# Transposing q on VectorE instead of TensorE in a pooled-attention and mixture-of-experts kernel

## The chip, the cores and the metric

The kernel runs on one core of a Trainium2 chip. The core has four compute engines: TensorE (PE in the profile, with its weight loads as PEld), VectorE (DVE), ScalarE (ACT) and GpSimd (POOL). A fifth one, SyncE (SP), issues nearly all transfers between the main memory and the on-chip memory (SBUF); 16 DMA engines carry them out. Matmul results go to eight banks of PSUM, 2 KB per partition each.

The metric is the time of one execution on the device in microseconds (us). Runs of this kernel before the change took 172.65, 172.67 and 173.02 us.

## What is computed

Batch 8, 8 heads, 576 tokens, 64 values a head. Attention with pooled keys and values feeds a layer of four attention experts, of which each token uses two. Shortened:

```python
# attention: 576 queries against 72 pooled keys
k_p = k.reshape(B, H, 72, 8, 64).mean(axis=3)
v_p = v.reshape(B, H, 72, 8, 64).mean(axis=3)
attn = softmax(q @ k_p.T / 8)
x = heads_side_by_side(attn @ v_p)            # (8, 576, 512)
# experts: causal attention in each, two experts a token by the gate
logits = x @ w_gate                           # (8, 576, 4)
for e in range(4):
    q, k, v = x @ wq[e], x @ wk[e], x @ wv[e]
    ye = softmax(causal(q @ k.T / 8)) @ v @ wo[e]
    out += gate_weight[e] * ye                # 0 where e is not among the two
```

## The kernel before

Each batch's 576 tokens are split into 512 main tokens and a tail of 64; the tails of two batches are put together in one tile of 128 rows. Work is cut into small units, each a function, named `batch:unit`. A text of names (`ORDER`, line 21) is the order in which the units are emitted, and every engine runs its instructions in that order. A unit can yield: its first appearance in the text emits its matmuls, the next one what reads their result (an exponential, a copy), and a third one what follows. So the text fixes the order within every engine's queue and, by the order of allocation, who gets which buffer.

The units of one batch, in the order of the data:

- `lk`, `lq`, `lv` load k, q, v of the main tokens (lines 312 to 319), four tokens to a partition, all eight heads, 1 MB each; batch 0 loads in four pieces and batch 1 in two (`CUTS`, line 77). `lkt`, `lqt`, `lvt` load the tails (lines 321 to 337). q's tails of two batches go into one tile, `qtail`.
- `ks`, `vs` add pairs of tokens (`sums`, on GpSimd or VectorE), `kp` and `vp` finish the pooling with a constant matrix on TensorE (`pool_k`, `pool_v`). `kp` leaves pooled keys with the 64 values of two heads in the 128 partitions, 72 pooled tokens in the columns.
- `qc` casts q to bf16 (`cast_q`, line 354): GpSimd from batch 2 on, VectorE and ScalarE for batches 0 and 1.
- `q0` to `q3` (`q_t`, line 396), one for each pair of heads: four TensorE transposes of 128x128 into a PSUM tile of the pool `ps1`, then a VectorE copy to `qT`. Batches 6 and 7 (`COPY_IN_ORDER`) reorder tokens in that copy.
- `s0` to `s3` (`scores`, line 419), one for each pair of heads: two matmuls that contract 64 rows each, in the upper and the lower half of the array, into one two-bank tile of the pool `ps2`; then one ScalarE exponential of 72x1024 into `etA`.
- `a0` to `a3` (`av`): the exponentials times the pooled values, and the division on VectorE, into `x_tm`. `x0` to `x3` (`x_t`) transpose that on TensorE against `perm`, an identity with its columns reordered, since the tokens come four to a partition. Batches 6 and 7 let DMA transpose (`xd`).
- `p` and `v` project to the experts' queries, keys and values, `g1` to `g6` make the gate weights, `c..` are the experts' scores and exponentials, `o` their outputs, `t` transposes, `w`, `y`, `z` the output projection and the store.
- Odd batches have a part for the two tails (`part_t`, line 756): `qt` casts q's tails on GpSimd, `qx` transposes them on TensorE, `sx` makes 16 score matmuls of 64 rows and 64 columns into one `ps2` tile and one exponential, and then `ax`, `xx`, `pt`, `vx`, `hd`, `h0`, `h1`, `ox`, `tx`, `w4` follow like the main units.
- `W:l.` and `W:c.` load and cast the weights. `W:h0` to `W:h31` (`busy`, line 287) are 32 pairs of matmuls on zeros whose result nobody reads.

`ps1` has two buffers of one bank, `ps2` three of two banks; together they are all of PSUM. `ps2` serves the scores of both attentions, the products with the values and `v`; `ps1` serves everything else. A unit that takes a buffer waits until the last reader of its former content is done.

Of the kernel before, what the change touches and what calls it, by code (L numbers as in the profile page):

```python
# [8 lines left out]
FP32 = mybir.dt.float32  # L9
BF16 = mybir.dt.bfloat16  # L10
ADD = mybir.AluOpType.add
# [10 lines left out]
W:h21 W:h22 W:h7 0:lk3 W:h3 0:lq3 0:lkt 0:ks3 0:kt 0:qc3d 0:lk2 W:h18 0:lk0 W:h14 W:h16 0:lv1 W:h27  # L22
0:lvt 0:qc3a W:h28 0:lq0 W:h13 0:kp3 0:lq2 0:lk1 W:h30 0:q3 0:vs1 1:lq1 0:lq1 0:kp3 0:qc0a 1:lkt
0:ks2 W:h12 W:h25 0:vt 1:qc1a 0:qc0d 0:lv2 0:q3 0:s3 0:qc2a W:h4 0:s3 0:qc1a 0:vs2 0:ks0 0:kp2 W:h9
W:h1 0:kp2 0:ks1 1:qc1d 0:qc2d 0:kp0 0:lv3 W:h26 0:kp1 0:kp0 W:h19 0:lv0 W:h15 0:kp1 0:q0 0:vs0 W:h5
0:qc1d 0:q2 0:q0 1:lq0 W:h8 0:q2 1:kt 0:vs3 0:q1 1:q2 0:q1 0:s0 0:s1 0:s0 0:s2 1:lk1 0:vp 1:q2 0:s2
1:lk0 1:lvt 0:vp 1:ks1 0:lqt W:h23 1:lv1 1:q3 0:a0 1:lv0 0:a2 1:q3 W:lk 1:qc0d 1:ks0 1:lqt W:h6 0:s1
0:a1 1:vt W:lq 0:a2 0:a0 1:qc0a 0:a1 W:h29 1:q1 W:h11 W:h17 W:h2 1:q1 1:kp1 1:kp0 1:kp1 1:vs0 1:kp0
0:a3 1:q0 0:a3 1:s2 1:qt 1:s1 1:q0 W:lv 0:x0 1:s0 1:s2 0:x2 2:lq 1:s1 1:s3 2:qc 1:s0 0:x0 W:c1 0:x2
0:x1 W:h10 W:h0 1:vs1 W:h20 W:h24 1:s3 0:x3 0:x1 1:vp 0:x3 W:c3 0:p1 2:lkt 1:vp W:c2 0:p1 1:qx 1:qx  # L30
1:a1 1:a3 1:a0 W:c0 0:p3 1:a1 1:sx 1:a3 0:p3 W:cv 2:kt 0:p0 1:a0 2:lk 1:a2 0:p2 0:v2 1:a2 1:sx 0:v0
0:p0 1:x3 0:p2 0:c2 1:x1 0:v2 0:c2 0:c11 0:v0 1:x3 1:x2 0:c11 0:c2 0:c10 1:x1 2:lv 2:lvt 1:x2 0:g1
0:c00 0:g2 0:c11 2:q0 2:q0 1:x0 1:x0 1:ax 2:q1 2:q1 1:ax 1:p1 1:p2 0:c00 0:c01 2:ks 3:lk 0:g3 0:g4
1:v2 3:lkt 1:p1 2:q3 1:v2 2:vs 2:q3 1:p2 2:lqt 2:kp 0:c01 1:v0 3:lqt 1:xx 2:kp 0:g5 3:lq 2:vt 3:lvt
2:s1 0:c10 0:c10 1:xx 2:s1 1:v0 2:s0 2:q2 1:vx 2:q2 2:s0 2:s3 2:s3 0:g6 2:s2 2:s2 3:lv 2:vp 4:lq
0:c00 1:vx 1:g1 0:o1 1:g2 2:vp 1:p3 2:a1 1:g3 2:a2 0:o1 3:ks 3:qt 0:c01 2:a1 1:p3 1:pt 2:a2 4:lkt
2:a0 1:p0 3:kt 1:pt 2:a3 2:a0 2:a3 4:lk 4:lvt 3:qx 1:g4 1:hd 1:h0 3:qx 3:qc 1:p0 1:hd 3:kp 1:h0
1:c11 3:kp 1:c2 2:x2 2:x1 3:vs 2:x2 3:vt 4:lv 1:c11 2:x1 0:o0 1:c2 2:x0 0:o0 2:x3 1:c00 2:x0 3:sx
2:x3 1:c00 1:c10 3:q2 3:q3 3:sx 2:v2 4:qc 3:q2 3:q3 0:t1 5:lq 1:c10 1:g5 3:q1 0:t1 4:kt 3:q1 3:s3
2:v2 2:v0 0:t0 2:v0 3:s3 3:s1 3:s2 0:t0 3:q0 3:s1 1:h1 3:vp 3:q0 2:p1 3:s2 1:hd 4:lqt 3:vp 3:s0  # L40
7:lkt 1:c01 4:q2 2:g1 1:h1 2:g2 1:c00 2:p1 4:q2 3:s0 3:a1 5:lkt 2:p0 4:q1 1:c2 3:a1 4:ks 4:q1 3:a3
2:p0 3:ax 2:p3 1:c11 1:c01 2:p3 3:a3 4:q3 2:c01 4:vt 2:c00 5:lk 1:c01 2:c01 4:q3 4:q0 3:ax 2:p2 1:g6
3:a0 4:q0 3:a0 5:lqt 4:kp 2:p2 4:kp 3:a2 4:vs 2:c00 1:ox 5:qc 3:xx 1:c10 3:a2 3:xx 4:s1 4:s0 1:o0
3:x1 1:ox 3:x3 3:x1 4:s1 3:x3 W:lo 4:s3 4:s0 4:s3 3:x0 4:vp 3:x0 5:ks 3:pt 3:pt 4:s2 4:vp 5:kt 2:c11
4:s2 3:x2 2:c00 5:q2 2:g3 1:o0 3:x2 2:c11 1:o1 3:p3 4:a3 5:q2 5:q3 3:p3 3:hd 5:lv 5:lvt 1:o1 2:c2
# [24 lines left out]
5:y2 7:c10 5:y2 7:pt 5:y1 5:y2 7:c2 7:c01 7:pt 5:y0 7:o1 7:g5 5:w4 7:c01 5:y0 7:g6 7:h1 5:w3 7:o1  # L70
7:c00 6:y1 5:w3 6:y1 7:c00 7:o0 6:w0 7:h1 7:t1 7:h0 5:y0 7:o0 5:w3 7:t1 7:hd 6:w0 7:t0 6:y1 7:hd
# [12 lines left out]
COPY_IN_ORDER = (6, 7)  # L84


@with_exitstack
def kernel(
    ctx: ExitStack,
    tc: tile.TileContext,  # L90
    q: bass.AP,
    k: bass.AP,
    v: bass.AP,
    moe_w_gate: bass.AP,
    moe_wq: bass.AP,
    moe_wk: bass.AP,
    moe_wv: bass.AP,
# [6 lines left out]
    POOLW = 8  # L104
# [917 lines left out]
```

## Time and profile before

| | |
|---|---|
| median of three runs | 172.67 us (172.65 to 173.02) |
| span of the profiled execution, first to last instruction | 171.8 us |
| HBM read, written | 30.42 MB, 9.44 MB |
| transfers | 52712 packets, 21712 of them under 512 B |
| TensorE, VectorE, ScalarE, GpSimd busy | 160.6, 124.3, 125.1, 100.8 us |

A profile is taken from one execution, whose instructions span a little less than the time that is measured for the run. Rows of instructions start with their start and length in microseconds, then engine, line, operation, `output<-inputs`, shapes and `x` the number of instructions merged in the row; in brackets stands how long the engine had been idle before, and what ended that. All instructions carry the line of the helper that emits them, L134, so they are told apart by their tiles. Rows of groups give the busy time and the mean of one instruction in ns, then the idle time before them and who ended it.

TensorE's rows need care: matmuls are pipelined, and each is shown with its whole latency. A matmul of 128 columns is shown with 219 ns. What it costs in a stream is the time from its start to the start of the next.

### The profile page before, as it was taken

How to read it: one execution, taken by the hardware profiler on the slowest of the kernel's cores; microseconds unless marked ns; L12 is line 12 of the kernel's file. 1: busy time of each engine (PE TensorE's matmuls, PEld its weight loads, DVE VectorE, ACT ScalarE, POOL GpSimd, SP SyncE). 2: the span in 40 equal slices, each digit the busy share in tenths (PEclk: the TensorE clock that was granted, in tenths of full speed). 3: DMA queues.
4: the chain of work that ended last, by engine and by line, in shares of the span. 5: the costliest groups of instructions: out<-in, count | busy, mean ns of one | idle time of the engine just before them, and what ended most of it. 6: DMA issues, size and time to landing. Idle time of an engine off the chain costs nothing.

```text
span 171.8 us, 5246 instructions
## 1 busy us (share of the span) xinstructions
PE 160.6 (94%) x2064; PEld 101.7 (59%) x2090; DVE 124.3 (72%) x358; ACT 125.1 (73%) x176; POOL 100.8 (59%) x222
## 2 busy tenths in 40 slices
PE   7968999899999999999999999999999999999990
PEld 2424544465767756777677667765665767456550
DVE  6465695858588786888768887878688658657861
ACT  2004717878787978679989759985998797798841
POOL 8402643157999969999962996891234133668200
PEclk9999999999999999999999999999999999999999
DMA  4999999999999999999939967641348355576966
GB/s 140 262 342 335 306 301 257 332 335 329 216 321 347 332 332 301 295 287 334 302 82 341 360 216 201 230 126 61 67 122 275 65 125 156 210 216 132 333 253 208
DMA packets 52712, 42.03 MB, mean 245 GB/s; under 512 B 21712, under 2 KB 47824, under 8 KB 52688
## 3 DMA queue, kind: packets, MB, share of 16 engines
q1 hardware_dynamic: 52608, 41.57, 82.8%
q8 instruction: 16, 0.26, 0.7%
q10 hardware_dynamic: 80, 0.13, 0.4%
q14 instruction: 8, 0.07, 0.2%
HBM read 30.42 MB, written 9.44 MB: 232 GB/s over the span
## 4 chain that ended last, share of the span: by engine, by line
PE 75%; DVE 7%; ACT 6%; DMA 4%; SPq 3%; issue 2%; DVEq 0%; ACTq 0%
PE p_ps L134 14%; PE v_ps L134 8%; PE y_ps L134 7%; PE sB_ps L134 5%; PE oB_ps L134 5%; PE sA_ps L134 4%; PE qT_ps L134 4%; DMA qraw<-in_q_dram 4%; PE idle_ps L134 4%; PE oA_ps L134 4%; PE xT_ps L134 3%; SPq L134 3%; PE oBt_ps L134 3%; PE vp_ps L134 2%; PE pt_ps L134 2%
## 5 line engine op out<-in xcount | busy, mean ns | idle before, releaser
L134 ACT ACTIVATE etA<-sA_ps 72x1024 bf16<-72x1024 f32 x32 | 31.3, 1018 | 10.7 <-PE sA_ps L134 10.5
L134 PE MATMUL p_ps<-xT,wqk 128*128 128x512 bf16 x114 | 31.5, 379 | 1.5 <-ACT qk L134 0.6
L134 ACT ACTIVATE etB<-sB_ps 128x1024 bf16<-128x1024 f32 x32 | 32.2, 1025 | 0.2 <-PE sB_ps L134 0.2
L134 POOL TENSOR_SCALAR_AFFINE_SELECT etB<-etB 128x256 bf16<-128x256 bf16 x48 | 18.8, 410 | 12.2 <-ACT etB L134 11.8
L134 POOL TENSOR_TENSOR vsum<-vraw 128x512 bf16<-128x512 f32 (+2 forms) x18 | 18.3, 1041 | 9.9 <-DMA vraw<-in_v_dram 9.8
L134 ACT CAST qk<-p_ps 128x512 bf16<-128x512 f32 x32 | 18.5, 586 | 7.6 <-PE p_ps L134 6.8
L134 DVE TENSOR_TENSOR x_tm<-oA_ps,rzA 128x512 bf16<-128x512 f32 x32 | 22.1, 692 | 1.1
L134 PE MATMUL idle_ps<-idle 128*128 128x512 bf16 x61 | 18.2, 414 | 3.1 <-DVE kp L134 1.3
L134 PEld LDWEIGHTS <-wqk 128*128 128x128 bf16 x192 | 14.7, 98 | 10.4 <-issue 1.1
L134 DVE COPY qT<-qT_ps 128x512 bf16<-128x512 bf16 x32 | 15.4, 487 | 6.2 <-PE qT_ps L134 5.9
L134 POOL TENSOR_TENSOR ksum<-kraw 128x512 bf16<-128x512 f32 (+1 forms) x16 | 18.0, 1146 | 2.3 <-DMA kraw<-in_k_dram 2.3
L134 PE MATMUL y_ps<-wo_t,oT 128*128 128x512 bf16 x57 | 16.7, 379 | 0.2
L134 PE MATMUL v_ps<-wvg,xT 128*128 128x260 bf16 x128 | 16.8, 274 | 0.0
L134 ACT COPY ofin<-y_ps 128x512 f32<-128x512 f32 x20 | 11.6, 587 | 6.4 <-PE y_ps L134 1.7
L134 POOL CAST qbf<-qraw 128x2048 bf16<-128x2048 f32 x6 | 11.4, 1897 | 5.6 <-ACT etT L134 5.5
L134 PEld LDWEIGHTS <-xT 128*128 128x128 bf16 x128 | 11.9, 97 | 3.1 <-issue 0.4
L134 PEld LDWEIGHTS <-etA 72*128 72x128 bf16 x256 | 11.0, 97 | 4.3 <-DVE x_tm L134 0.4
L134 PE MATMUL sB_ps<-qk 64*128 64x512 bf16 (+3 forms) x128 | 13.2, 299 | 0.0
L134 PEld LDWEIGHTS <-etB 128*128 128x128 bf16 x256 | 11.3, 97 | 2.5 <-POOL etB L134 0.6
L134 DVE COPY xT<-xT_ps 128x512 bf16<-128x512 bf16 x24 | 9.7, 420 | 4.1 <-PE xT_ps L134 3.8
L134 PE MATMUL oB_ps<-vaug,etB 128*128 128x65 bf16 x256 | 12.4, 193 | 0.1
L134 PE MATMUL qT_ps<-ident,qbf 128*128 128x128 bf16 x128 | 12.2, 219 | 0.3
(125 smaller groups left out, 329.8 us busy)
## 6 DMA issues: line engine op xcount, KB each, us to landing
out_dram<-ofin SPq DMA_DIRECT2D x28, 256.0 KB, 2.7
qraw<-in_q_dram SPq DMA_DIRECT2D x6, 1024.0 KB, 9.9
kraw<-in_k_dram SPq DMA_DIRECT2D x6, 1024.0 KB, 9.8
vraw<-in_v_dram SPq DMA_DIRECT2D x6, 1024.0 KB, 8.2
kraw<-in_k_dram SPq DMA_DIRECT2D x4, 256.0 KB, 4.9
qraw<-in_q_dram SPq DMA_DIRECT2D x4, 256.0 KB, 5.4
ktail<-in_k_dram SPq DMA_DIRECT2D x8, 128.0 KB, 7.1
vraw<-in_v_dram SPq DMA_DIRECT2D x4, 256.0 KB, 6.2
```

The costliest lines, as they stand in the source:

```text
L134: return tc.keep_in_program_order(fn(*args, **kwargs))
```

## The change

- q is loaded with 18 consecutive tokens to a partition, for all 576 tokens: 32 partitions hold one head, 128 partitions four heads, and the eight heads make two halves, `h2`. The separate load of q's tail, its cast `qt`, its transpose `qx` and the tile `qtail` go.
- The cast writes bf16 with the values of two consecutive tokens side by side, so that a pair makes one 32-bit word. From batch 2 on it is two GpSimd instructions of 1152 elements; in batches 0 and 1 VectorE takes five ninths and ScalarE four ninths.
- The TensorE transposes and VectorE copies of `q0` to `q3` become one VectorE transpose of 32x32 blocks of those words, 1152 words a partition (two of 576 in batches 0 and 1). It leaves the tokens in order. `qT` has three buffers, and the tails read it too.
- The keys are laid out alike: in each quarter of the partitions 32 of a head's 64 values, the other 32 in a second tile index `x`. `pool_k` keeps 12 matmuls a batch.
- `scores` has two units a batch, `s0` and `s1`, of four heads each: eight matmuls of 32 rows on the four row groups, into two `ps2` tiles, four that start and four that add up; then two exponentials in two further steps. The tail scores `sx` have 32 matmuls instead of 16, two `ps2` tiles and two exponentials of half the size.
- `x_t` uses `ident`; `perm` goes. Batch 0 loads k, v, q in two pieces. The zeros of `busy` are read with a repeated 128-column pattern. A scratch tile of the set-up is placed in a buffer of `otp`.
- `ORDER` is written anew, 861 names instead of 966. Six of the `W:h` units stand behind the last output unit.

```diff
@@ ORDER: the first lines of each, and the last
-W:h21 W:h22 W:h7 0:lk3 W:h3 0:lq3 0:lkt 0:ks3 0:kt 0:qc3d 0:lk2 W:h18 0:lk0 W:h14 W:h16 0:lv1 W:h27
-0:lvt 0:qc3a W:h28 0:lq0 W:h13 0:kp3 0:lq2 0:lk1 W:h30 0:q3 0:vs1 1:lq1 0:lq1 0:kp3 0:qc0a 1:lkt
...
-6:w0 6:y3 7:h0 7:hd 7:t0 6:y3 7:z2 6:y3 7:z2 7:ox 7:ox 6:w2 6:w2 7:z0 7:tx 6:w2 7:tx W:h31 7:w4 7:z0
-7:w4 7:w4
+0:lq1 0:lkt 0:lk1 0:ks1 W:h18 W:h3 0:lq0 W:h2 0:qc0a W:h4 0:lv1 0:lvt W:h19 W:h7 W:h9 0:kt W:h25
+0:lv0 0:qc1a 1:lq1 W:h13 0:vt 1:lkt W:h16 0:qc1d W:h10 0:q1 0:vs0 W:h30 W:h21 0:lk0 0:qc0d W:h22
+1:qc1a 0:kp1 1:lk1 W:h29 0:kp1 1:lk0 W:h31 0:q0 1:lq0 0:vs1 0:ks0 0:s1 0:vp 1:kt 1:lv0 0:kp0 W:lq
+0:s1 2:lkt 1:ks1 0:kp0 0:s0 1:lvt 1:qc1d 0:vp W:h15 0:s1 1:lv1 0:a2 1:q1 0:a2 0:s0 1:ks0 0:a0 0:s0
+W:h14 1:kp1 0:a0 1:qc0d W:h0 0:a1 0:a3 2:kt 1:kp1 0:a1 W:lk 1:kp0 0:a3 1:vt W:h11 0:x2 1:s1 1:qc0a
+W:c0 1:s1 1:kp0 0:x0 0:x2 W:h12 1:q0 1:vs0 W:lv 0:x3 0:x3 2:lq 0:x0 1:s1 1:vs1 1:sx 0:x1 0:x1 1:sx
+1:s0 1:vp 0:p0 1:vp 1:sx 1:s0 2:lk 1:s0 W:c1 1:a1 2:qc 1:ax W:c3 W:h27 W:cv 1:a1 1:a3 1:a0 2:ks
...
+6:w2 7:h0 7:hd 7:t1 7:h0 7:t0 6:y3 7:t1 6:y3 6:w0 7:hd 7:z2 6:y1 6:y3 7:z2 6:y1 7:ox 7:ox 7:z0 6:y1
+7:tx 7:tx 7:z0 7:w4 7:w4 W:h17 W:h23 W:h26 W:h5 W:h8 W:h20
-CUTS = {0: 4, 1: 2}
+CUTS = {0: 2, 1: 2}
-QT_IN_ORDER = ()
-COPY_IN_ORDER = (6, 7)
...
+    QUAD = 32
+    NQ = S // QUAD
+    NJ = NQ // 2
...
-    idle = const.tile([128, 512], BF16, name="idle")
+    idle = const.tile([128, 128], BF16, name="idle")
...
-    kp_bufs = persistent("kp", 3, [128, NHP, 128], BF16, [(lambda t: t[:, :, SP:128], 0.0)])
+    kp_bufs = persistent("kp", 3, [128, 2, 2, 128], BF16, [(lambda t: t[:, :, :, SP:128], 0.0)])
...
+        def load_q(h2s):
+            if "q" not in raw:
+                raw["q"] = rawp.tile([128, 2, NQ * D], FP32, name="qraw", tag="qraw")
+            h0, h1 = 4 * h2s[0], 4 * h2s[-1] + 4
+            sp.dma_start(
+                out=raw["q"][:, h2s[0] : h2s[-1] + 1, :],
+                in_=q[b, h0:h1, :, :].rearrange(
+                    "(h2 i) (p r) d -> (i p) h2 (r d)", i=4, r=NQ
+                ),
+            )
...
+        def cast_q(h2s, j0, j1, eng):
             if "q" not in st:
-                st["q"] = sump.tile([128, NR, H, D], BF16, name="qbf", tag="qbf")
+                st["q"] = sump.tile([128, 2, NJ, D, 2], BF16, name="qbf", tag="qbf")
             copy = act.copy if eng is act else eng.tensor_copy
+            for h2 in h2s:
+                src = raw["q"][:, h2, :].rearrange("p (j two d) -> p j two d", two=2, d=D)
+                copy(
+                    out=st["q"][:, h2, j0:j1].rearrange("p j d two -> p j two d"),
+                    in_=src[:, j0:j1],
+                )
+
+        def q_t(h2s):
+            if "qT" not in st:
+                st["qT"] = apool.tile([128, 2, 2, S], BF16, name="qT", tag="qT", bufs=3)
+                qts[b] = st["qT"]
+            a, z = h2s[0], h2s[-1] + 1
+            words = st["q"][:, a:z].rearrange("p h j d two -> p (h j d two)").bitcast(FP32)
+            dve.transpose(
+                out=st["qT"][:, a:z].rearrange("p h x t -> p (h x t)").bitcast(FP32).rearrange(
+                    "p (hx i j) -> p j hx i", i=QUAD, j=NJ
+                ),
+                in_=words.rearrange("p (h j x d) -> p j h (x d)", h=z - a, j=NJ, x=2),
+            )
...
-        def scores(hp):
-            ps = ps2.tile([128, 2, MAIN], FP32, name="sA_ps", tag="ps2")
-            for hh in range(2):
-                r0 = hh * D
-                pe.matmul(
-                    out=ps[:, hh, :], lhsT=kp[r0 : r0 + D, hp, :],
-                    rhs=st["qT"][r0 : r0 + D, hp, :], start=True, stop=True,
-                )
-            yield
-            et = etp.tile([SP, 2, MAIN], BF16, name="etA", tag="etA")
-            act.activation(out=et[:], in_=ps[0:SP, :, :], func=EXP, scale=ATT_EXP_SCALE)
-            st["et"][hp] = et
+        def scores(h2):
+            ps = [ps2.tile([128, 2, MAIN], FP32, name="sA_ps", tag="ps2") for _ in range(2)]
+            for x in range(2):
+                for i in range(4):
+                    r = slice(QUAD * i, QUAD * i + QUAD)
+                    pe.matmul(
+                        out=ps[i // 2][:, i % 2, :], lhsT=kp[r, h2, x, :],
+                        rhs=st["qT"][r, h2, x, 0:MAIN], start=(x == 0), stop=(x == 1),
+                    )
+            for n in range(2):
+                yield
+                et = etp.tile([SP, 2, MAIN], BF16, name="etA", tag="etA")
+                act.activation(out=et[:], in_=ps[n][0:SP, :, :], func=EXP, scale=ATT_EXP_SCALE)
+                st["et"][2 * h2 + n] = et
...
         def scores():
-            ps = ps2.tile([128, 2, 2 * NHP, TAIL], FP32, name="sAt_ps", tag="ps2")
+            ps = [ps2.tile([128, 2, 512], FP32, name="sAt_ps", tag="ps2") for _ in range(2)]
             for i, b_ in enumerate(both):
+                for h2 in range(2):
+                    c = (i * 2 + h2) * TAIL
+                    for x in range(2):
+                        for n in range(4):
+                            r = slice(QUAD * n, QUAD * n + QUAD)
+                            pe.matmul(
+                                out=ps[n // 2][:, n % 2, c : c + TAIL],
+                                lhsT=kp_bufs[b_ % 3][r, h2, x, :],
+                                rhs=qts[b_][r, h2, x, MAIN:S], start=(x == 0), stop=(x == 1),
+                            )
```

More of the change, by code (lines that the diff above doesn't have):

```diff
@@ L298 @@
     units.update({"W:cv": cast_wv, "W:co": cast_wo})
-    pairs = {}
+    qts = {}
     def part_a(b: int):
@@ L362, in pool_k @@
-        def pool_k(p0, p1):
-            ps = ps1.tile([128, NHP, SP], FP32, name="kpT_ps", tag="ps1")
-            for hp in range(p0, p1):
-                for g in range(2):
+            for h2 in h2s:
[16 more added lines that the diff above has]
+            )
@@ L366, in pool_k @@
+        def pool_k(h2s):
+            ps = ps1.tile([128, 2, 2, SP], FP32, name="kpT_ps", tag="ps1")
+            for h2 in h2s:
+                hs = slice(4 * h2, 4 * h2 + 4)
+                for x in range(2):
+                    for g in range(2):
+                        pe.matmul(
+                            out=ps[:, h2, x, :], lhsT=st["k"][:, g, x, hs, :],
+                            rhs=pm[:, 0:SP], start=(g == 0), stop=False,
+                        )
                     pe.matmul(
-                        out=ps[:, hp, :], lhsT=st["k"][:, g, 2 * hp : 2 * hp + 2, :],
@@ L759, in part_t @@
         st = {}
-        def cast():
-            st["q"] = sump.tile([128, DM], BF16, name="qtb", tag="qtb")
-            pool.tensor_copy(out=st["q"][:], in_=pairs[b // 2][:])
-        def q_t():
-            ps = ps1.tile([128, NHP, 128], BF16, name="qTt_ps", tag="ps1")
-            for hp in range(NHP):
-                pe.transpose(
-                    out=ps[:, hp, :], in_=st["q"][:, hp * 128 : hp * 128 + 128],
-                    identity=ident[:],
-                )
-            yield
-            st["qT"] = apool.tile([128, NHP, 128], BF16, name="qTt", tag="qTt", bufs=1)
-            dve.tensor_copy(out=st["qT"][:], in_=ps[:])
```

224 lines of the change are left out of this document (90 added, 134 removed).

## The prediction

> **What bounds the kernel now.** I read the page first: the busy shares, the slices and the chain that ended last. The best of the 40 slices moves 361 GB/s.
>
> ```profile
> span 171.8 us, 5246 instructions
> ...
> PE 160.6 (94%) x2064; PEld 101.7 (59%) x2090; DVE 124.3 (72%) x358; ACT 125.1 (73%) x176; POOL 100.8 (59%) x222
> ...
> PEclk9999999999999999999999999999999999999999
> ...
> GB/s 140 262 342 335 306 301 257 332 335 329 216 321 347 332 332 301 295 287 334 302 82 341 360 216 201 230 126 61 67 122 275 65 125 156 210 216 132 333 253 208
> ...
> PE 75%; DVE 7%; ACT 6%; DMA 4%; SPq 3%; issue 2%; DVEq 0%; ACTq 0%
> ```
>
> TensorE (PE) runs at full clock throughout, holds three quarters of the chain and is busy 94% of the span. A busy PE in this profile is not yet a PE at its peak, so I looked next at the stretches behind the start, and then at single matmuls in order of time. The columns of the stretches are PE, weight load, VectorE (DVE), ScalarE (ACT), GpSimd (POOL), clock, DMA share, GB/s.
>
> ```profile
> 30.00:60.00 30.00, 28.78 (x405) 19.60 (x406) 22.60 (x68) 24.37 (x36) 22.38 (x40) 1.00 1.07 316
> 60.00:100.00 40.00, 39.48 (x577) 26.81 (x583) 31.82 (x90) 33.86 (x46) 33.19 (x56) 1.00 1.01 295
> 100.00:140.00 40.00, 39.34 (x537) 26.00 (x544) 30.66 (x88) 33.50 (x49) 20.60 (x51) 1.00 0.50 142
> ```
>
> From 30 us on PE has next to no idle time; ACT follows at 81 to 85% and POOL, between 60 and 100 us, at 83%. What a unit of matmuls costs there is read from the start of one row to the start of the next (first column), not from the busy time:
>
> ```profile
> 34.04 1.04 PE L134 MATMUL p_ps<-xT,wqk 128*128 128x512 bf16 x4
> 34.92 0.41 PE L134 MATMUL oA_ps<-vp,etA 72*128 72x65 bf16 x8
> ...
> 44.32 0.39 PE L134 MATMUL qT_ps<-ident,qbf 128*128 128x128 bf16 x4
> 44.54 0.23 PE L134 MATMUL kpT_ps<-pm,ksum 128*128 128x72 bf16 x2
> ...
> 45.83 0.39 PE L134 MATMUL xTt_ps<-ident,x_tt 128*128 128x128 bf16 x4
> 46.15 0.61 PE L134 MATMUL sA_ps<-qT,kp 64*128 64x512 bf16 x4
> 46.68 0.40 PE L134 MATMUL qT_ps<-ident,qbf 128*128 128x128 bf16 x4
> ...
> 57.42 0.41 PE L134 MATMUL sAt_ps<-qTt,kp 64*128 64x64 bf16 x16 [0.29 <-ACT etC L134]
> 57.66 0.39 PE L134 MATMUL sB_ps<-qk 64*128 64x512 bf16 x2
> ```
>
> A 512-column matmul costs (34.92 - 34.04)/4 = 0.22 us. Four transposes cost 44.54 - 44.32 = 0.22 us. Four score matmuls with 64 rows take 46.68 - 46.15 = 0.53 us; one after the other they would be 0.88, so two on different row halves run at once (0.44) and 0.09 is left over. The four transposes before them take 46.15 - 45.83 = 0.32 instead of 0.22. So a change of the array's height costs about 0.10 us, on entering and on leaving. Sixteen tail scores take 0.24 us.
>
> The start is bound otherwise: by when loads land.
>
> ```profile
> 27.59 1.42 POOL L134 TENSOR_TENSOR vsum<-vraw 128x256 bf16<-128x256 f32 x2 [3.61 <-DMA vraw<-in_v_dram]
> ```
>
> ```profile
> 29.39 0.62 ACT L134 CAST wqk<-vraw 128x512 bf16<-128x512 f32 x1 [1.25 <-DMA vraw<-in_moe_wk_dram]
> 31.59 0.62 ACT L134 CAST wqk<-vraw 128x512 bf16<-128x512 f32 x1 [0.15 <-DMA vraw<-in_moe_wq_dram]
> ```
>
> ```profile
> 30.07 1.04 PE L134 MATMUL p_ps<-xT,wqk 128*128 128x512 bf16 x4
> ```
>
> Batch 1's values land at 27.6 us, the two weights at 29.4 and 31.6, and the first projection starts at 30.07. Ahead of that PE fills up with idle matmuls:
>
> ```profile
> L134 PE MATMUL idle_ps<-idle 128*128 128x512 bf16 x61 | 18.2, 414 | 3.1 <-DVE kp L134 1.3 <-DVE idle L161 1.2 <-PE xT_ps L134 0.3
> ```
>
> So what the change saves of PE work there is worth nothing.
>
> **The change part by part**, each as microseconds of the path from the first projection to the end, which is PE's.
>
> *Transposes of q, removed.* Of 32 units of four, 8 (batches 0 and 1) stand ahead of the first projection. The other 24 and the 4 units of the tails (same shape) cost 28 x 0.22: **-6.2**.
>
> *Score matmuls.* Behind the first projection there were 24 units of two at 0.22; there will be 12 units of two groups of four, 32 rows each. If four run at once, a group costs 0.22 and the sum stays 5.3 us: **0**. No row shows 32-row matmuls. Bounds: 0, and +5.3 if only two run at once; I take 0, because the nearest rows, 64-row pairs, overlap fully. The Trainium skill ("TensorE: Matmul & The Clock Gate", Part 3, packing small matmuls) gives 3.07 times for four such tiles of 512 columns, not 4. By that the 24 groups would cost 24 x 0.22 x 0.30 = 1.6 us more, an estimate; no run here shows it yet.
>
> *Tail scores.* 16 matmuls become 32, on four row groups. Nearest row 0.24 us for 16, so 0.48 for 32; one of the four units moves ahead of the first projection: 3 x 0.48 - 4 x 0.24 = **+0.5** (bounds -0.2, if four groups make up for the count, and +2 at twice the price).
>
> *Changes of height.* A unit's matmuls are issued where its name first stands in the order. Between the first projection and the last output I count 83 changes in the old order and 100 in the new one (15 visits at 32 rows, 35 at 64): 17 x 0.10 = **+1.7** (bounds 0, where PE waits anyhow, and 3.4).
>
> *Idle units.* One of the old ones stands in that stretch (two matmuls), five of the new: 4 x 0.44 = 1.8 us if PE had work instead, 0 if it would wait. I take half: **+0.9**. Six more stand behind the last output: 12 x 0.22 = 2.6 us, from the end of its copies on. Their cover is the last store:
>
> ```profile
> 167.63 0.69 DVE L134 COPY ofin<-yt_ps 64x512 f32<-64x512 f32 x1 [0.19 <-PE yt_ps L134]
> ```
>
> 168.3 + 2.6 = 170.9, under the span's 171.8. So 0; without this cover it would be at most 1.
>
> *Start.* Adding up the loads in written order, 6.95 MB were issued up to batch 1's last values (landed 27.6) and 8.13 MB up to the second weight (31.5): 0.30 MB/us. The new order has 7.73 MB up to those values, hence 30.2 us at that rate. But its 2.36 MB of q come in 4.6 KB runs (18 tokens) instead of 1 KB and 256 B; at the page's best slice, 361 GB/s, they would save 1.3 us: 28.9. Behind the landing stand two sums, in the new kernel on DVE, and the pooled values:
>
> ```profile
> 27.00 0.75 DVE L134 TENSOR_TENSOR vsum<-vraw 128x256 bf16<-128x256 f32 x2
> ```
>
> ```profile
> 29.30 0.61 PE L134 MATMUL vp_ps<-vsum,pm 128*128 128x512 bf16 x2
> ```
>
> With 0.75 for the sums and 30.07 - 29.30 = 0.77 for the pooled values the first projection starts between 30.4 and 31.7, against 30.07: +0.3 to +1.6. I take **+0.5**, nearer the lower end, since the runs do get longer. SP issues 14 loads fewer (8 tails of q, and batch 0 in halves instead of quarters):
>
> ```profile
> 1.30 0.45 SPq L134 DMA_DIRECT2D qraw<-in_q_dram  x1
> ```
>
> That is about 14 x 0.45 us of SP's queue, but the two waits above end with a transfer, not with an issue: 0. Pooled k keeps its 12 matmuls a batch: 0.
>
> *Casts and copies off the path.* These rows carry them:
>
> ```profile
> L134 DVE COPY qT<-qT_ps 128x512 bf16<-128x512 bf16 x32 | 15.4, 487 | 6.2 <-PE qT_ps L134 5.9
> L134 DVE COPY ofin<-y_ps 128x512 f32<-128x512 f32 x8 | 5.5, 690 | 4.6 <-PE y_ps L134 3.9 <-PE pt_ps L134 0.6
> L134 DVE CAST vat<-vt_ps 128x256 bf16<-128x256 f32 x4 | 1.7, 418 | 0.0
> L134 POOL CAST qbf<-qraw 128x2048 bf16<-128x2048 f32 x6 | 11.4, 1897 | 5.6 <-ACT etT L134 5.5
> L134 POOL CAST qtb<-qtail 128x512 bf16<-128x512 f32 x4 | 2.4, 612 | 1.4 <-DMA qtail<-in_q_dram 1.3
> L134 ACT ACTIVATE etT<-sAt_ps 72x1024 bf16<-72x1024 f32 x4 | 4.1, 1019 | 0.0
> L134 ACT CAST qk<-p_ps 128x512 bf16<-128x512 f32 x32 | 18.5, 586 | 7.6 <-PE p_ps L134 6.8 <-remote 0.6 <-PE sB_ps L134 0.2
> L134 ACT ACTIVATE etA<-sA_ps 72x1024 bf16<-72x1024 f32 x32 | 31.3, 1018 | 10.7 <-PE sA_ps L134 10.5
> ```
>
> DVE transposes 1152 words a batch, a shape of work that no row shows. From 418 ns (256 elements) and 690 (512) one element costs 1.06 ns, hence 0.69 + 640 x 1.06 = 1.37 us, against 4 x 0.49 now: DVE loses about 0.6 us a batch. Upper bound, two cycles a word: 2.7 us. I take 1.37, as all single-rate rows lie on that line. The rule that speaks against it: the Trainium skill ("SBUF — State Buffer", section on the DMA port swizzle) says that each access that crosses to a new 16-byte line pays a penalty, and this write steps 36 bytes. By that page the transposes would lie towards the upper bound; no run here shows it yet.
>
> POOL's cast goes from 1.90 us plus half of 0.61 to two of 1152 elements; at (1897 - 612)/1536 = 0.84 ns an element each is 1.15 us, 2.3 against 2.2 a batch. Its output now steps over every second element; if that doubled it, POOL would have 2.3 us more a batch, in a stretch where it has 6.8 of 40 us free. ACT's tail exponential splits in two of half the size: by the 512-element row 2 x 0.59 against 1.02, +0.15 four times. All three lie beside PE, which hides them as long as scores are not waiting for q.
>
> *Waits.* The new scores take two of the three two-bank PSUM buffers (ps2) in one visit and wait until both are free; behind them in PE's queue stands everything else. In return 28 transposes leave ps1, which has two buffers. Bounds from -1.5 to the first rival's price; I take **+0.4**.
>
> Sum: -6.2 + 0 + 0.5 + 1.7 + 0.9 + 0.5 + 0.4 = -2.2: a span of 169.6. The median of the runs is 172.67, 0.9 above this profile's span, so **170.5 us**; without surprises between 168.5 and 172.5.
>
> **Rivals.**
>
> *Two PSUM buffers at once (slower).* Each of the 15 visits behind the first projection waits for a second ps2 buffer, whose reader is mostly an exponential of 1.02 us. At half of one, 15 x 0.51 = 7.6 us: 170.5 - 0.4 + 7.6 = **177.7**. It turns the sign from (172.7 - 170.1)/15 = 0.17 us a visit. For it: ACT is busy 85% in the middle, so readers come late. Against it: today ACT has 6 of 40 us to spare, and the transposes' buffers are gone.
>
> *Row groups do not run four at once (the change does not do what it says).* With pairs alone +5.3: **175.8**; it turns the sign from 2.2/24 = 0.09 us a group. By the 3.07 of the Trainium skill ("TensorE: Matmul & The Clock Gate", Part 3) it would be 172.1. For it: four streams and four weight loads compete where today's rows show two. Against it: no loss is seen with two.
>
> *The transposes are slow and late.* At 2.7 us instead of 1.4, if each of six batches' scores waits for the difference: 6 x 1.3 = 7.8, **178.3**. Against it: q is cast well ahead, and DVE is busy only 75 to 80% of those stretches.
>
> *More is gained.* The idle units stand only where PE would wait (-0.9), half of the added height changes too (-0.8), and fewer ps1 buffers save 1.5 instead of costing 0.4 (-1.9): **166.9**.
>
> **How the numbers follow.** Forecast 0.45, two buffers 0.17, row groups 0.10, slow transposes 0.08, more gained 0.20. Faster by over 0.2% (0.35 us, about what a measurement of this kernel can tell): nearly all of the forecast (0.42), all of the last case, and 0.03 of the milder forms of the others: 0.65. Within 0.2%: 0.06, at the forecast's upper end. Slower: 0.29. The range takes in the last rival to 165.5 and the slower ones up to 177; about 0.17 is left out, most of it above.
>
> **What would show it.** Right: no qT_ps and qTt_ps on PE, the interval of a group of four 32-row matmuls near 0.22 us, the DVE transpose near 1.4 us, about 50 visits at less than full height behind the first projection, that one near 30.6 us, and etA's exponentials starting without a longer wait. Wrong: PE idle before sA_ps with ACT etA or etB as its releaser (two buffers), intervals of 0.4 us a group (row groups), DVE qT above 2 us with scores behind it, POOL casts of q above 2 us each, or a first projection later than 31.7 us.

## The result and the profile after

The changed kernel takes 173.69 us (median of 20 runs, 173.10 to 174.82), the one before 173.04 in runs beside it (20 runs, 172.57 to 174.38). The ratio is 1.0042 with a 95% interval of 1.0024 to 1.0061: slower by about 0.4%, where 170.5 us had been forecast.

The page of the changed kernel: span, busy times, TensorE's clock in 40 slices, and shares of the chain.

```profile
span 171.4 us, 5199 instructions
...
PE 157.4 (92%) x2074; PEld 93.0 (54%) x2074; DVE 125.8 (73%) x321; ACT 125.5 (73%) x178; POOL 101.5 (59%) x222
...
PEclk9997599999999999999999999999999999999999
...
PE 51%; DVE 17%; ACT 14%; DMA 5%; issue 5%; POOL 4%; SPq 3%; DVEq 0%; ACTq 0%; POOLq 0%
```

TensorE has less to do, as forecast, yet its share of the chain fell from 75 to 51%, and VectorE's rose from 7 to 17%. So TensorE now waits. How much, the stretch from 30 to 110 us shows, in which the transposes of batches 2 to 7 lie. The columns are PE, weight load, DVE, ACT, POOL, clock, DMA share, GB/s. First the kernel before, from a run of it made for comparison (c0 below), then the changed one.

```profile
30.00:110.00 80.00, 79.55 (x1133) 53.76 (x1131) 63.73 (x184) 65.84 (x91) 63.54 (x112) 1.00 1.00 291
```

```profile
30.00:110.00 80.00, 76.13 (x1071) 47.59 (x1070) 66.75 (x164) 65.69 (x93) 69.26 (x114) 1.00 0.86 278
```

PE's idle time went from 80 - 79.55 = 0.45 us to 3.87. DVE, which was to lose work, has 3.0 us more in this stretch. The view of PE's waits from 30 to 112 us in the changed kernel names who was waited for (total us, times, longest):

```profile
PE xT_ps L127 <- DVE xT L127: 1.8, 2, 1.3
PE oA_ps L127 <- ACT etA L127: 0.6, 2, 0.3
PE sB_ps L127 <- ACT etA L127: 0.5, 2, 0.3
PE oA_ps L127 <- DVE vaug L127: 0.4, 1, 0.4
PE idle_ps L127 <- DVE oT L127: 0.4, 1, 0.4
PE sA_ps L127 <- ACT qk L127: 0.4, 1, 0.4
PE sB_ps L127 <- DVE x_tm L127: 0.2, 1, 0.2
```

VectorE's instructions (`xT`, `vaug`, `oT`, `x_tm`) hold 2.8 of these 4.3 us, ScalarE's the rest. The longest wait, in order of time, first on PE and then on DVE:

```profile
37.83 0.40 PE L127 MATMUL xT_ps<-ident,x_tm 128*128 128x128 bf16 x4
39.57 0.38 PE L127 MATMUL xT_ps<-ident,x_tm 128*128 128x128 bf16 x4 [1.34 <-DVE xT L127]
```

```profile
36.68 0.41 DVE L127 COPY xT<-xT_ps 128x512 bf16<-128x512 bf16 x1
37.01 2.26 DVE L127 STREAM_TRANSPOSE qT<-qbf 128x1152 f32<-128x1152 f32 x1
39.11 0.41 DVE L127 COPY xT<-xT_ps 128x512 bf16<-128x512 bf16 x1
```

The new transpose of batch 2 starts at 37.01 us and takes 2.26. The copy behind it in DVE's queue frees a buffer of `ps1` for which PE has been standing since 39.57 - 1.34 = 38.2. Nobody needs the transposed q yet; it is batch 1's `xT` that comes late. The groups that answer to the prediction's rows, from the view that keeps shapes apart:

```profile
L127 POOL CAST qbf<-qraw 128x1152 bf16<-128x1152 f32 x12 | 17.3, 1484 | 7.2 <-DMA qraw<-in_q_dram 7.2
...
L127 DVE STREAM_TRANSPOSE qT<-qbf 128x1152 f32<-128x1152 f32 x6 | 13.7, 2276 | 0.8 <-POOL qbf L127 0.8
...
L127 DVE STREAM_TRANSPOSE qT<-qbf 128x576 f32<-128x576 f32 x4 | 4.8, 1210 | 1.2 <-ACT qbf L127 1.2
L127 ACT ACTIVATE etT<-sAt_ps 72x512 bf16<-72x512 f32 x8 | 4.3, 591 | 0.3 <-PE sAt_ps L127 0.2
```

(2276 - 1210)/576 = 1.85 ns a word, where 1.06 was assumed.

### The profile page after: what moved, and what is told of

Its sections match the earlier page's. It is cut to its first block, busy times and chain, and to the rows that moved or that the text cites. A ratio compares the mean times of both kernels' runs of the same rounds, so it can differ in the third digit from the quotient of the medians.

```text
span 171.4 us, 5199 instructions
## 1 busy us (share of the span) xinstructions
PE 157.4 (92%) x2074; PEld 93.0 (54%) x2074; DVE 125.8 (73%) x321; ACT 125.5 (73%) x178; POOL 101.5 (59%) x222
## 4 chain that ended last, share of the span: by engine, by line
PE 51%; DVE 17%; ACT 14%; DMA 5%; issue 5%; POOL 4%; SPq 3%; DVEq 0%; ACTq 0%; POOLq 0%
PE p_ps L127 9%; ACT etA L127 8%; PE y_ps L127 6%; DVE x_tm L127 5%; DMA kraw<-in_k_dram 5%; PE v_ps L127 5%; DVE qT L127 5%; PE sB_ps L127 5%; PE oB_ps L127 4%; PE oA_ps L127 3%; SPq L127 3%; PE idle_ps L127 3%; PE sA_ps L127 3%; PE oBt_ps L127 2%; ACT qk L127 2%
## 5 line engine op out<-in xcount | busy, mean ns | idle before, releaser
L127 PE MATMUL p_ps<-xT,wqk 128*128 128x512 bf16 x128 | 32.6, 379 | 0.0
L127 POOL CAST qbf<-qraw 128x1152 bf16<-128x1152 f32 x12 | 17.3, 1484 | 7.2 <-DMA qraw<-in_q_dram 7.2
L127 PE MATMUL idle_ps<-idle 128*128 128x512 bf16 x64 | 19.1, 434 | 2.2 <-DVE idle L154 1.0
L127 DVE STREAM_TRANSPOSE qT<-qbf 128x1152 f32<-128x1152 f32 (+1 forms) x10 | 18.5, 1850 | 2.0 <-ACT qbf L127 1.2
L127 POOL TENSOR_TENSOR vsum<-vraw 128x512 bf16<-128x512 f32 (+1 forms) x16 | 17.8, 1135 | 1.7 <-DMA vraw<-in_v_dram 1.7
L127 PE MATMUL y_ps<-wo_t,oT 128*128 128x512 bf16 x64 | 18.3, 380 | 0.1
L127 PE MATMUL sB_ps<-qk 64*128 64x512 bf16 (+3 forms) x128 | 13.9, 300 | 0.7 <-ACT etA L127 0.5
L127 PE MATMUL oA_ps<-vp,etA 72*128 72x65 bf16 x256 | 12.6, 197 | 1.0 <-ACT etA L127 0.6
L127 PE MATMUL sA_ps<-qT,kp 32*128 32x512 bf16 x128 | 10.9, 394 | 2.8 <-DVE kp L127 2.3
```

The source lines that it names most:

```text
L127: return tc.keep_in_program_order(fn(*args, **kwargs))
```

## The experiments

The theory: the transpose is slow because of how it writes, and the time that it takes on VectorE makes copies late that TensorE waits for. Rivals: ScalarE and the `ps2` buffers, the idle units, something outside the span, the slower cast of q.

**e2: the transpose writes dense**

```diff
-                    "p (hx i j) -> p j hx i", i=QUAD, j=NJ
+                    "p (hx j i) -> p j hx i", i=QUAD, j=NJ
```

> The changed kernel with one edit: VectorE's transpose writes its 32-bit words one after the other instead of every ninth (36 bytes apart). The tokens of q then stand in another order than in the reference; every instruction and its size stay. Theory (the stepped write makes the transpose slow, and copies behind it on VectorE come late to TensorE): the 1152-word transpose falls from 2.28 us to 1.2 to 1.5 us, TensorE's waits of 7.1 us fall by 1.5 to 3 us, and the time falls by 1.5 to 3 us. Rival (the waits come from ScalarE and the ps2 buffers, and VectorE has slack): the transpose falls as well, the time by less than 0.5 us. Rival (the transpose is slow however it writes, 4-byte words being the cause): it stays above 2 us and the time stays.

Measured: 170.86 us, ratio to before 0.9870 (0.9843 to 0.9898), 2.83 us under the changed kernel. Groups, the same stretch, and PE's waits in it:

```profile
L127 DVE STREAM_TRANSPOSE qT<-qbf 128x1152 f32<-128x1152 f32 x6 | 8.2, 1372 | 1.4 <-POOL qbf L127 1.4
...
L127 DVE STREAM_TRANSPOSE qT<-qbf 128x576 f32<-128x576 f32 x4 | 3.1, 768 | 1.0 <-ACT qbf L127 1.0
```

```profile
30.00:110.00 80.00, 78.21 (x1135) 49.18 (x1136) 64.88 (x174) 67.50 (x95) 69.86 (x114) 1.00 0.86 278
```

```profile
PE oA_ps L127 <- ACT etA L127: 0.6, 2, 0.3
PE xT_ps L127 <- DVE xT L127: 0.5, 1, 0.5
PE sB_ps L127 <- DVE x_tm L127: 0.2, 1, 0.2
PE sB_ps L127 <- ACT etA L127: 0.2, 1, 0.2
PE sAt_ps L127 <- ACT etA L127: 0.2, 1, 0.2
```

1372 ns is the 1.37 us that the prediction had taken. PE's idle time in the stretch falls from 3.87 to 1.79 us; the waits for `vaug` and `oT` are gone, the one for `xT` falls from 1.8 to 0.5. What is left is mostly ScalarE's, so that rival is small. The theory holds: one stepped address pattern costs 2.8 us, more than the gain of 2.2 that had been forecast.

**e10: dense, and VectorE's time given back**

```diff
+            if z - a > 1:
+                dve.transpose(out=<half 0 of qT, dense>, in_=<half 0 of words>)
```

> The dense write of all batches (tokens of q in another order than in the reference), and in batches 2 to 7 VectorE transposes the first half a second time right behind, 0.76 us each. If it is VectorE's time that cost the 2.8 us between this kernel without the repeat (170.86) and the changed one, most of it comes back: 172.5 to 173.7 us. If the stepped write did its harm in another way (holding GpSimd off the memory, say), the time stays near 170.9.

Measured: 174.07 us, ratio 1.0083 (1.0055 to 1.0110): all of it is back. Six repeats of 0.775 us, 4.65 in all, cost 174.07 - 170.86 = 3.2 us, 0.7 for each microsecond of DVE. (The stepped write of the same six batches takes 6 x (2276 - 1372) ns = 5.4 us more than the dense one and costs 2.8, 0.5 for each.) The two transposes together (2.18 us here) make the same wait at the same place as the one of 2.26:

```profile
37.53 2.18 DVE L127 STREAM_TRANSPOSE qT<-qbf 128x1152 f32<-128x1152 f32 x2
39.64 0.39 DVE L127 COPY xT<-xT_ps 128x512 bf16<-128x512 bf16 x1
```

```profile
40.08 0.38 PE L127 MATMUL xT_ps<-ident,x_tm 128*128 128x128 bf16 x4 [1.32 <-DVE xT L127]
```

So VectorE's time alone is enough to bring back the whole loss; the stepped write need not do harm in another way, and no wait shows one. Batches 0 and 1 stayed dense here, so their four transposes ahead of the first projection had no share in e10's loss.

**e8: the same work in two halves**

```diff
+            for n, h2 in enumerate(h2s if b < 6 else h2s[::-1]):
...
+                if n == 0 and len(h2s) > 1:
+                    yield
```

with a second `b:q` seven or eight names behind the first.

> The changed kernel, with the transpose of batches 2 to 7 cut into two of 576 words, the second one some eight units later in the order; same stepped write, same work, about 0.14 us more on VectorE a batch. Theory in its narrow form (what hurts is that one long instruction stands ahead of copies that TensorE needs): each such wait is cut by up to 1.1 us, and the time falls by 1 to 2 us. Rival (VectorE has too much to do in those stretches, whoever stands where): the time stays within 0.5 us.

Measured: 173.68 us, ratio 1.0037 (1.0014 to 1.0061), no gain. The narrow form of the theory falls. The four largest of PE's waits in this kernel:

```profile
PE v_ps L136 <- DVE o_sc L136: 1.2, 2, 0.6
PE oA_ps L136 <- ACT etA L136: 0.6, 2, 0.3
PE xT_ps L136 <- DVE xT L136: 0.5, 1, 0.5
PE oA_ps L136 <- DVE vaug L136: 0.4, 1, 0.4
```

The wait for `xT` fell to what it is with the dense write, but 1.2 us of waits for `o_sc` are new. Other work of VectorE is late instead. That is what the rival foretold: it isn't one long instruction at an unlucky place, but too much for DVE to do in this stretch, wherever it stands.

**e1, e3, e12: the idle units**

```diff
-7:tx 7:tx 7:z0 7:w4 7:w4 W:h17 W:h23 W:h26 W:h5 W:h8 W:h20
+7:tx 7:tx 7:z0 7:w4 7:w4
```

That is e1. e3 takes away `W:h27`, `W:h28`, `W:h1`, `W:h6` and `W:h24` too, and e12 is e3 with e2's dense write.

> The changed kernel without the six idle units behind the last output unit; the twelve matmuls that nobody reads no longer end the program. The changed kernel's run is 1.7 us longer than its span and the one before about 0.9 us longer than its own; if TensorE still working while the last store lands is what costs this, the time falls by 0.5 to 1.0 us and the run is again about 0.9 us longer than its span. If the slow transposes and the waits behind them are all of it, these units lie beside the store (issued at 167.7 us, about 2.6 us to land) and the time changes by less than 0.3 us.

> The changed kernel without the six trailing idle units and without the five that stand behind the first projection, 0.44 us each on TensorE. If TensorE has other work ready at those places, the time falls by up to 2.2 us more than without the trailing six alone. If it would wait there (theory: it waits for copies behind VectorE's transposes), by 0.5 us or less.

> The dense write of all batches (tokens of q in another order than in the reference), without the six trailing idle units and the five behind the first projection. In the changed kernel taking these eleven away gained nothing, but there TensorE waited for VectorE's late copies. The prediction put the five at 0.9 us (half of their time; all of it is 2.2 us). If they cost that once VectorE is in time, this kernel takes 169.3 to 170.2 us; if TensorE would wait for something else at those places anyway, 170.7 to 171.1, as with the dense write alone (170.86).

Measured: 173.73 us (1.0045, 1.0025 to 1.0066), 173.94 (1.0052, 1.0030 to 1.0074) and 171.20 (0.9887, 0.9858 to 0.9916). None is faster than its counterpart with the units, 173.69 and 170.86. The six trailing units lie beside the last store, as the prediction had it; by these times the five others stand where PE would wait, with the slow transposes and with the quick ones. e1's run is 1.7 us longer than its span, as the changed kernel's.

**c0: the kernel before, time and span of one run**

> The kernel before as it is, to have its span and its time from one and the same run. If its run is about 0.9 us longer than its span, the 1.7 us of the changed kernel are 0.8 us of loss outside the span; if it is 1.7 us too, nothing is lost there, and the spans compare as the times do.

Measured: 173.01 us (10 runs); the profiled one took 172.47 with a span of 170.8, 1.7 more. In the changed kernel's 20 runs the difference is 1.66 to 1.79. So nothing is lost outside the span. The 0.9 of the prediction compared a span with runs that it did not belong to: if 1.7 holds for it too, that profile was of a longer execution, of about 171.8 + 1.7 = 173.5.

**e11: the cast of q written dense**

```diff
-                src = raw["q"][:, h2, :].rearrange("p (j two d) -> p j two d", two=2, d=D)
+                src = raw["q"][:, h2, :].rearrange("p (j n) -> p j n", j=NJ)
                 copy(
-                    out=st["q"][:, h2, j0:j1].rearrange("p j d two -> p j two d"),
+                    out=st["q"][:, h2, j0:j1].rearrange("p j d two -> p j (d two)"),
```

> The changed kernel with one edit: the casts of q write one value after the other instead of every second (the values of q then stand in other places than in the reference). If the step costs GpSimd, its cast of 1152 elements falls from 1.48 us to 1.0 to 1.2 us, the 1.15 us that were forecast. Theory: GpSimd is not what TensorE waits for, and the time changes by less than 0.4 us; rival: earlier casts let VectorE's transposes start earlier, and the time falls by 0.5 to 1.5 us.

Measured: 173.45 us, ratio 1.0031 (1.0009 to 1.0054), which cannot be told from the changed kernel. The cast itself falls to the forecast:

```profile
L127 POOL CAST qbf<-qraw 128x1152 bf16<-128x1152 f32 x12 | 13.4, 1148 | 6.9 <-DMA qraw<-in_q_dram 6.9
...
L127 DVE CAST qbf<-qraw 128x640 bf16<-128x640 f32 x4 | 1.9, 483 | 0.0
```

GpSimd has 3.9 us less to do, and nothing comes of it: it isn't what TensorE waits for.

**e4, e5, e7, e9: a write that is quick and in order**

For a dense write that keeps the order of the tokens, neighbouring words of the output must come from neighbouring partitions, so q has to be loaded two tokens to a partition at a time (e4). The other three write with a shorter step (e7, e9), or leave the order to TensorE's read (e5):

```diff
@@ e4, batches 2 to 7: 2 tokens, dense write, one transfer a head
+                        out=raw["q"][r, h // 4, :].rearrange("p (j n) -> p j n", j=NJ),
+                        in_=q[b, h, :, :].rearrange("(j p two) d -> p j (two d)", p=QUAD, two=2),
@@ e5: 16 tokens and 2 for the tail, dense write, TensorE reads in steps
+                        out=raw["q"][:, h2, c],
+                        in_=q[b, 4 * h2 : 4 * h2 + 4, t0:t1, :].rearrange("i (p r) d -> i p (r d)", r=r),
+                        rhs=st["qT"][r, h2, x, 0:MAIN].rearrange("p (j i two) -> p i j two", i=QUAD, two=2), ...
@@ e7: 4 tokens and 2 for the tail, write with a step of 8 bytes, transfers as in e5 for each 128 tokens
+                    out=to[:, :, 0 : MAIN // 2].rearrange("p x (gi r2) -> p r2 x gi", r2=2),
+                    in_=words[:, 0 : 8 * D].rearrange("p (g rx d) -> p rx g d", g=4, d=QUAD),
@@ e9, batches 2 to 7: as e7, one transfer a head and four for the tails
+                        in_=q[b, h, 0:MAIN, :].rearrange("(g p r) d -> p g (r d)", g=4, r=4),
```

> A form of the dense write that keeps the reference's order, from batch 2 on: q is loaded with two tokens to a partition and block (runs of 512 bytes instead of 4608), in eight transfers of one head each instead of one; then the dense write leaves the tokens in order. Batches 0 and 1 are as in the changed kernel. Theory: the transposes of six batches fall to 1.2 to 1.5 us and the time by 1.2 to 2.5 us, less what 42 more transfers on SyncE's queue and nine times as many packets of q cost; if the transfers come late, 'qraw' shows as what POOL's casts wait for, and the gain is gone. Rival (VectorE has slack): no gain, or a loss by the transfers.

> q's 512 main tokens are loaded 16 to a partition and its 64 tail tokens 2 to a partition (four transfers a batch instead of one, runs of 4096 and 512 bytes), the transpose writes dense, and the score matmuls put the tokens in order by reading qT in steps (2 values, then 128 bytes further); all that is computed stays. Theory: the transposes take 1.4 us as with the dense write alone and the time is 1.5 to 3 us under the changed kernel's, if TensorE reads in steps as fast as it reads dense (sA in groups of 8 at 0.54 us). Rival: the step that slowed VectorE's write slows TensorE's read too; at twice the time a matmul the 16 visits cost 16 x 0.44 = 7 us more, a time of about 178. Rival: more transfers make q late, as in the two-token load (there POOL's casts waited 15.7 us for qraw).

> q's main tokens are loaded 4 to a partition and stretch of 128 (runs of 1024 bytes, ten transfers a batch instead of one), so that the in-order write of the transpose steps 8 bytes instead of 36; three to four instructions a batch instead of one; all that is computed stays. It prices the step: if a step within 16 bytes costs nothing, a transpose of 512 words takes about 0.70 us (0.61 us a thousand words dense: 1.37 us for 1152) and the time falls by 1 to 2.5 us against the changed kernel; if every step costs, it takes about 1.1 us as at 36 bytes (1.21 us for 576 words) and the time stays or rises. Rival: the ten transfers of shorter runs make q late and the time rises by some us whatever the transpose does.

> The write with a step of 8 bytes again (q four tokens to a partition and stretch of 128), from batch 2 on, but with transfers whose outermost dimension is the 32 partitions of a head instead of the four heads: eight of 128 KB and four tails a batch. Batches 0 and 1 are as in the changed kernel. In the run before, a word of the 8-byte step took as long as a dense one, and its transfers ran at a quarter of the rate, with about four of the sixteen DMA engines' worth of work at a time. If that came from the outermost dimension of four, the transfers are as quick as in the kernel before and the time falls to 171 to 172.5 us, by the theory; if it came from the many transfers, the time stays above 180.

Measured: 183.6 us (ratio 1.0609, 1.0559 to 1.0659), 242.9 (1.404, 1.398 to 1.410), 244.6 (1.410, 1.404 to 1.416) and 190.1 (1.0966, 1.0908 to 1.1024). All are slower, and what the views show points at their transfers, though no run took the transfers alone. In e4 the DMA engines are full, but the slices in which most of batches 2 to 7's q is loaded, in runs of 512 bytes, move 182 to 239 GB/s, where the changed kernel has 314 and more in every slice from 4 to 77 us:

```profile
DMA  5999999999999999999999999014334966446885
GB/s 162 368 340 356 347 326 204 209 327 336 182 202 185 325 339 239 207 334 353 346 222 234 214 329 365 24 29 118 89 120 116 207 130 186 154 143 182 291 298 171
```

(The 15.7 us of waits for `qraw` that e5's expectation takes from e4 are POOL's only to 5.1; 10.6 are ScalarE's, in batches 0 and 1.) But e5 and e7 each price a step. In e7 the transposes with 8 bytes from word to word run at the dense rate:

```profile
L127 DVE STREAM_TRANSPOSE qT<-qbf 128x512 f32<-128x512 f32 x16 | 11.3, 706 | 33.4 <-POOL qbf L127 25.2 <-ACT qbf L127 8.2
```

By the two dense rows of e2, 512 words would take 768 - 64 x (1372 - 768)/576 = 701 ns. (The 0.61 us in e7's expectation is about the 0.60 between these rows, for 576 words, not for a thousand; its 0.70 us is right.) In e5 TensorE's eight score matmuls, reading in steps of 128 bytes, take 131.21 - 130.25 = 0.96 us, at a granted clock of 1.00:

```profile
130.25 1.03 PE L127 MATMUL sA_ps<-qT,kp 32*128 32x512 bf16 x8
131.21 1.04 PE L127 MATMUL p_ps<-xT,wqk 128*128 128x512 bf16 x4
```

In the changed kernel they take 55.32 - 54.78 = 0.54. So TensorE's read is slowed by steps as well.

The transfers of e5 and e7 have the four heads as their outermost dimension, and moved at most 356 GB/s, mostly far less, with the DMA engines half empty at the start. The 40 slices of e5, in tenths and GB/s:

```profile
DMA  2665686862894322993499733339503239654896
GB/s 59 127 176 135 175 216 195 199 220 105 220 310 155 118 98 104 250 334 122 130 265 356 237 121 118 120 130 286 214 3 88 90 110 180 147 147 142 235 315 221
```

This was not isolated any further. The Trainium skill ("DMA: Bandwidth & Descriptors", section on why a DMA increments its semaphore by 16) says that a transfer is spread over the largest number of engines, up to 16, that divides the outermost dimension of both of its sides: with four heads on one side and 128 partitions on the other, four engines. From 54 to 163 us, the slices of e5 that move 98 to 130 GB/s show 2 to 4 tenths of the 16 engines busy, which agrees. e9 has 32 outermost and is 54 us quicker than e7 with more transfers a batch, which agrees too, though batches 0 and 1 differ as well. What was left in e9 stays open: its transfers are more and their runs shorter than the changed kernel's, and neither was tried alone. SyncE's queue is taken up for 9.65 us by the twelve of one batch and for 5.78 by those of the next, where the changed kernel's one takes 1.35. From the timelines of e9 and of the changed kernel:

```profile
42.11 9.65 SPq L127 DMA_DIRECT2D qraw<-in_q_dram  x12
```

```profile
39.23 1.35 SPq L127 DMA_DIRECT2D qraw<-in_q_dram  x1
```

POOL's casts wait 20.2 us for `qraw` in e9, and 7.2 in the changed kernel. None of the four beats the kernel before. A form that writes dense, keeps the order and loads q in one transfer was not found; it would have to come near e2's 170.9.

## Why the prediction was wrong

The step that failed is *casts and copies off the path*: "I take 1.37, as all single-rate rows lie on that line." Those rows write dense, this transpose doesn't. It took 2.28 us, inside the bounds (2.7) and on the side to which the quoted rule pointed.

The second failure follows from it: "All three lie beside PE, which hides them as long as scores are not waiting for q." The condition named the wrong victim. Between 30 and 112 us no score waits for `qT`; what waits is the work that needs the copies standing behind the transpose in VectorE's queue. That made *waits* +3.4 us of PE's idle time between 30 and 110 us instead of +0.4.

The path from the first projection (the first `p_ps`) to the last output projection (the last `yt_ps`) shows both at once. In order: the kernel before (c0), the changed kernel, and e2; the columns are those of the stretches.

```profile
30.00:165.84 135.84, 135.06 (x1898) 88.98 (x1895) 103.83 (x301) 112.20 (x159) 86.97 (x181) 1.00 0.82 238
```

```profile
29.09:166.32 137.23, 132.21 (x1874) 81.83 (x1872) 103.66 (x279) 112.94 (x163) 90.77 (x183) 1.00 0.75 231
```

```profile
29.11:163.51 134.40, 131.89 (x1875) 81.74 (x1873) 99.00 (x279) 112.89 (x163) 90.67 (x183) 1.00 0.77 236
```

These three executions compare: they took 172.47, 173.10 and 170.30 us, each 0.5 to 0.6 under the median of its kernel. The profile that the prediction read, of a longer execution, has 166.89 - 30.07 = 136.8 us here, and its trace holds only 114 of the 128 `p_ps` matmuls.

PE's busy time on the path fell by 135.06 - 132.21 = 2.9 us, where the terms of PE's own work, -6.2 + 0.5 + 1.7 + 0.9, make -3.1: about right. Its idle time rose from 0.8 to 5.0 us, by 4.2, where *waits* had +0.4. So the sum without its start, -2.2 - 0.5 = -2.7, came out at 137.23 - 135.84 = +1.4. The dense write alone takes 2.8 us off the path, of the 4.1 by which that sum was off.

With the dense write the path is 1.4 us shorter than before, half of what was forecast: the idle time is still 1.7 us longer, and the idle units fill four times 0.44 us more in which, by e12, PE would have waited. That e2's 170.86 us come so near to the 170.5 of the forecast is therefore partly luck: the path falls short by 1.3 us, and the start, 0.9 us earlier where 0.5 later was forecast, makes up for it.

The other terms:

- *Score matmuls* 0 and *changes of height* 0.10 each: right. The traces of c0 and of the changed kernel have 82 and 99 changes on the path, 17 more, as forecast. From the changed kernel, eight matmuls of 32 rows, and 32 tail scores, to the start of the next row:

```profile
54.78 0.61 PE L127 MATMUL sA_ps<-qT,kp 32*128 32x512 bf16 x8 [0.39 <-ACT qk L127]
55.32 0.62 PE L127 MATMUL vt_ps<-wvg,xTt 128*128 128x260 bf16 x4
...
56.74 0.41 PE L127 MATMUL sAt_ps<-qT,kp 32*128 32x64 bf16 x32
57.08 1.04 PE L127 MATMUL p_ps<-xT,wqk 128*128 128x512 bf16 x4
```

  0.54 = 2 x 0.22 + 0.10: four row groups at once and one change of height. Eight of the twelve visits behind the first projection take this, the other four 0.58 to 0.73. The 3.07 times of the Trainium skill ("TensorE: Matmul & The Clock Gate", Part 3), by which two groups would cost, as an estimate, 0.57 without the change, is not what this trace shows.
- *Tail scores* +0.5: too high. The unit shown takes 0.34 us with the change of height behind it, so about 0.24 without, instead of 0.48; of the three behind the first projection two take this, the third 0.52.
- *Idle units* +0.9: taking them away gains nothing (e3, e12). The six trailing ones: 0, as forecast (e1).
- *Start* +0.5: wrong in sign. The first projection starts at 29.09 instead of 30.07, or 30.00 in c0. Batch 1's last values are being summed from 27.24 us on, where 28.9 had been taken as the earliest landing. From 4.3 to 30 us the slices move 314 to 370 GB/s, where the profile before has 257 to 342.
- POOL's cast 1.15 us: 1.48, between the bounds and without effect (e11). ACT's tail exponential 0.59: 591 ns.
- The 0.9 between span and run: 1.7 for either kernel (c0).

Of the rivals, two buffers at once did not come: no `sA_ps` waits for `etA` or `etB` from 30 to 112 us, and within the twelve visits the matmuls into the second buffer start at most 0.19 us behind the first ones. Nor did pairs of row groups. *The transposes are slow and late* named the cause, at 0.08, but priced it with six batches' scores at 7.8 us; other work paid, and less than half. "DVE is busy only 75 to 80%" was no argument against it: at 81 to 83% in this stretch, 0.5 to 0.7 us were lost for each added one (e2, e10).

## What to carry to other kernels

Price an instruction from rows with the same address pattern: a step between the words of its output made this one two thirds longer, although count, type and engine were the same. Work moved to an engine that isn't the bound is hidden only if nobody stands behind it in that engine's queue; here, with that engine 81 to 83% busy, half and more of the added time was lost. If a layout is mended at the load, count the transfers, and look at their outermost dimension and at the length of their runs. And when a corrected run meets the forecast, check the terms: here two errors cancelled.

## What the runs showed of the hardware

- A 32x32 transpose on VectorE takes 1.05 ns a 32-bit word with a dense write ((1372 - 768)/576), about 1.1 with a step of 8 bytes ((706 - 202)/448, with e7's instructions of 64 words), 1.85 with 36. The Trainium skill ("SBUF — State Buffer", section on the DMA port swizzle) has free steps within a line of 16 bytes and a penalty beyond; these three agree, the casts of the next item, which step 4 bytes, do not.
- A cast to bf16 that writes every second element, 64 at a time, costs GpSimd 1484 ns instead of 1148, VectorE 864 instead of 483 (640 elements) and ScalarE 760 instead of 615 (512).
- TensorE reading its moving operand two values at a time, 128 bytes apart, runs at about half rate: 0.96 instead of 0.54 us for the eight score matmuls, at a granted clock of 1.00 in both.
- TensorE's granted clock fell in the head of the changed kernel, where TensorE had little to do. Its stretch from 10 to 20 us, and that of the kernel before (c0):

```profile
10.00:20.00 10.00, 5.16 (x44) 2.04 (x43) 7.83 (x13) 4.05 (x5) 4.86 (x8) 0.75 1.09 358
```

```profile
10.00:20.00 10.00, 9.23 (x79) 4.62 (x77) 5.68 (x20) 4.94 (x8) 2.91 (x7) 1.00 1.10 337
```

  PE is busy 5.2 instead of 9.2 of 10 us, and the clock is 0.75 instead of 1.00. Whether the lower clock cost anything was not tried; the first projection starts earlier than in the kernel before all the same.
